# A decode kernel's final store: one transfer of four rows, or two of two rows from two queues

## The chip, the cores and the metric

The kernel runs on one core of a Trainium2 chip. The metric is the device time of one execution in microseconds (us), lower is better; every run quoted as timed was repeated in rounds with the kernel before on the same chip.

Short names used below: PE is TensorE, DVE is VectorE, ACT is ScalarE, POOL is GpSimd, SP is SyncE. "SPq" and "ACTq" are the sequencers of SP and ACT, on which the profile records the issues of DMA transfers. The "record" of an issue is the time that the issuing instruction takes on its sequencer in the profile; a "packet" is one entry of the profile's DMA records (the store of before has four of 512 B); a "count" is one recorded increment of a transfer's semaphore (that store has five).

## The reference, cut to what matters

One decoded token goes through layernorm, and then two branches are added: grouped-query attention over a cache of 65,536 positions, and a small mixer with an MLP. Only the last line, its shape and its size matter here: one row of 1024 bf16 numbers, 2 KB.

```python
x = A_x                                   # (1, 1, 1024)
xn = _layernorm(x, axis=-1)
return x + _A_ref(xn, A_k_cache, A_v_cache, A_wq, A_wo) + _B_ref(xn, B_w1, B_w2, B_w3, B_w4)
```

## The kernel before

Every operation is recorded in a queue for its engine, with the semaphores that it must wait for. `_dma` records a transfer on the queue that issues it; the kernel takes the channel's n-th transfer as done when the channel's semaphore has reached 16 * n. `q_sp.wait` makes SP wait.

```python
def _dma(q, chan, fn, reads=(), writes=(), partial=False):
    _deps(q, reads, writes)               # waits of the issuing queue
    chan.n += 1
    ev = q.dma(fn, chan.sem, 16 * chan.n) # issued by q; "done" is sem >= 16 * n
    _done(ev, reads, writes, partial)
    return ev
```

All final terms are summed in one PSUM tile, `OUT_ps`: the 1024 outputs lie as four rows of 256 in partitions 0, 32, 64 and 96, because the kernel writes each product of one row as four matmuls, each with a `tile_position` of its own.

```python
def out_rows(items, reads, last=False):
    ...
        for jj in range(4):
            ... e.matmul(OUT_ps[32 * jj:32 * jj + 1, 0:256], lhs, rhs[:, 256 * jj:256 * jj + 256],
                         start=False, stop=last, tile_position=(0, 32 * jj), skip_group_check=True)
```

The end of the program waits for the four parts of the weight w4 in turn, adds them, casts the sum to bf16 in `orow`, and stores its four rows with one transfer:

```python
for i in range(len(w4_parts)):
    w4_pe(i)                              # last part: 2 rows of w4, 8 matmuls
_op(q_dve, lambda e: e.tensor_copy(orow[:, :], OUT_ps[:, 0:256]), reads=[b_OUT], writes=[b_orow])
ev_out = _dma(q_sp, chan("out"), lambda e: e.dma_start(
    out=out[0, 0, :].rearrange("(j n) -> j n", j=4), in_=orow[0:97:32, :]), reads=[b_orow])
q_sp.wait(ev_out)
```

ACT issues one transfer in the whole program before the change, the load of x at its start.

## Time and profile before

| | before |
|---|---|
| median of 6 runs | 403.74 us (403.67 to 404.6) |
| span in the profile | 401.93 us |
| HBM read | 169.87 MB at 423 GB/s |
| start of the store's issue to end of span ("the tail") | 2.06 us |

These lines of the page show what bounds the kernel. "DMA" gives the busy share of the DMA engines in 40 equal slices of the span, in tenths.

```profile
span 401.9 us, 5169 instructions
PE 193.7 (48%) x2059; PEld 83.0 (21%) x2059; DVE 227.8 (57%) x400; ACT 48.3 (12%) x127; POOL 61.8 (15%) x90
...
DMA  8999999999999999999999999999999999999994
...
HBM read 169.87 MB, written 0.00 MB: 423 GB/s over the span
```

The DMA engines are busy 90% or more from the second slice to the last but one; no other engine passes 57% of the span. The change touches none of that. What it touches is seen in the chain of waits that ended last (start, length, what):

```profile
374.69 24.24 DMA Kn<-in_B_w_dram
398.93 0.04 issue
398.98 0.42 PE OUT_ps L392 x8
399.39 0.02 issue
399.42 0.42 DVE orow L619
```

and in the timeline of the end (start, length, engine, line, operation):

```profile
399.42 0.42 DVE L619 CAST orow<-OUT_ps 128x256 bf16<-128x256 f32 x1 [13.16 <-PE OUT_ps L392]
399.87 0.65 SPq L620 DMA_DIRECT2D out_dram<-orow  x1
```

The last load lands, eight matmuls and the cast follow, and then there is only the store, over 2 us of it although it moves 2 KB. A table of short windows shows when bytes move in that time; the last two columns are the busy share of the DMA engines and GB/s.

```profile
400.20:401.10 0.90, 0.00 (x0) 0.00 (x0) 0.00 (x0) 0.00 (x0) 0.00 (x0) 1.00 0.00 0
401.10:401.25 0.15, 0.00 (x0) 0.00 (x0) 0.00 (x0) 0.00 (x0) 0.00 (x0) 1.00 0.06 14
401.25:401.50 0.25, 0.00 (x0) 0.00 (x0) 0.00 (x0) 0.00 (x0) 0.00 (x0) 1.00 0.00 0
```

Only the window from 401.10 to 401.25 holds packets. The trace has every packet and every count that arrives at the store's semaphore. Written out from those records, with times from the start of the span:

```
399.870  SP issues the store (record 0.645 us)
400.893  first count: the one that comes ahead of all data
401.120, 401.140, 401.148, 401.180   packets of 512 B, 25 or 26 ns each
401.470, 401.489, 401.498, 401.534   four counts, 0.26 to 0.33 us after the end of the last of these packets
401.551  SP goes on
401.932  end of span, after the closing barrier
```

So 1.25 us pass from the issue to the first packet, 0.09 with packets, 0.33 to the last count, 0.02 to SP and 0.38 in the barrier.

### The profile page before, as it was taken

The page shows a single profiled execution, that of the slowest core. Times are in us where ns is not written, and L with a number is a line of the kernel's source. Part 1 is how long each engine was busy: PE and PEld are TensorE (multiplying, and loading weights), DVE is VectorE, ACT ScalarE, POOL GpSimd, SP SyncE. Part 2 cuts the span into 40 slices and gives each one's busy share as a digit, 9 for nine tenths or more (in the row PEclk, how much of TensorE's full clock was granted, in tenths as well). Part 3 has the DMA queues.
Part 4 walks back from the last instruction along what each step waited for, and adds up shares of the span by engine and source line. Part 5 has one row for each costly group of instructions (what it writes and reads, how often), then busy time and mean ns, then how long its engine had stood idle before and what let it go on. Part 6 is the DMA issues. An engine that isn't in the chain of part 4 may idle for free.

```text
span 401.9 us, 5169 instructions
## 1 busy us (share of the span) xinstructions
PE 193.7 (48%) x2059; PEld 83.0 (21%) x2059; DVE 227.8 (57%) x400; ACT 48.3 (12%) x127; POOL 61.8 (15%) x90
## 2 busy tenths in 40 slices
PE   0361446064525756286640965454443645445645
PEld 0250111021103511062110731121111311111232
DVE  0217666277816588255753388576836775788410
ACT  0000201012101011011110011111201111111200
POOL 5000013011211011110310102111110112112110
PEclk9999999999955565555565556565565855665686
DMA  8999999999999999999999999999999999999994
GB/s 356 427 416 436 444 421 419 450 432 421 444 434 423 432 434 439 416 434 452 423 420 450 426 424 444 432 421 435 430 435 427 445 430 424 424 431 430 436 419 205
DMA packets 7088, 170.20 MB, mean 423 GB/s; under 512 B 916, under 2 KB 920, under 8 KB 1048
## 3 DMA queue, kind: packets, MB, share of 16 engines
q1 hardware_dynamic: 6920, 169.87, 98.4%
q8 instruction: 16, 0.26, 0.2%
q14 instruction: 8, 0.07, 0.0%
q10 hardware_dynamic: 144, 0.00, 0.0%
HBM read 169.87 MB, written 0.00 MB: 423 GB/s over the span
## 4 chain that ended last, share of the span: by engine, by line
DMA 54%; DVE 22%; PE 17%; ACT 3%; issue 2%; SPq 0%; POOL 0%; ACTq 0%
DMA Kn<-in_A_k_cache_dram 43%; DVE X L464 11%; DMA Kn<-in_B_w_dram 6%; DMA Vn<-in_A_wq_dram 5%; PE H_ps L367 4%; DVE pT_f L517 3%; PE S_ps L476 3%; PE OT_ps L524 3%; DVE mrow L483 3%; ACT p_sb L506 3%; PE M_ps L367 2%; PE PT_ps L515 2%; PE M_ps L552 1%; PE OUT_ps L392 1%; DVE Yall L381 1%
## 5 line engine op out<-in xcount | busy, mean ns | idle before, releaser
L464 DVE STREAM_TRANSPOSE X<-Kn 128x1024 f32<-128x1024 f32 x128 | 151.7, 1215 | 64.2 <-DMA Kn<-in_A_k_cache_dram 64.2
L524 PE MATMUL OT_ps<-Vn,pT_f 128*32 128x512 bf16 x512 | 59.9, 620 | 27.2 <-DVE pT_f L517 27.2
L476 PE MATMUL S_ps<-X,Yall 128*32 128x512 bf16 x512 | 57.5, 593 | 17.0 <-DVE X L464 17.0
L489 PE MATMUL MB_ps<-Rm,Lmat 128*128 128x16 bf16 x32 | 6.1, 192 | 87.3 <-DVE Rm L484 87.3
L538 POOL TENSOR_TENSOR O_acc<-O_acc,tmpO 128x513 f32<-128x513 f32 x28 | 32.9, 1174 | 89.0 <-ACT tmpO L532 89.0
L506 ACT ACTIVATE p_sb<-S_ps,brun 128x512 bf16<-128x512 f32 x32 | 22.0, 687 | 172.3 <-DVE brun L504 153.8
L536 POOL TENSOR_SCALAR O_acc<-O_acc,ff 128x513 f32<-128x513 f32 x28 | 19.5, 698 | 149.8 <-ACT ff L511 149.8
L515 PE MATMUL PT_ps<-p_sb,permR 128*128 128x512 bf16 x32 | 18.2, 568 | 39.7 <-ACT p_sb L506 39.7
L483 DVE TENSOR_REDUCE mrow<-S_ps 128x1 f32<-128x512 f32 x32 | 21.6, 674 | 24.2 <-PE S_ps L476 24.2
L532 ACT ACTIVATE tmpO<-OT_ps 128x512 f32<-128x512 f32 x32 | 19.1, 598 | 107.6 <-PE OT_ps L524 107.6
L476 PEld LDWEIGHTS S_ps<-X,Yall 128*32 128x32 bf16 x512 | 16.5, 125 | 54.8 <-DVE X L464 38.6
L517 DVE STREAM_TRANSPOSE pT_f<-PT_ps 128x512 f32<-128x512 f32 x32 | 22.9, 716 | 7.6 <-PE PT_ps L515 7.6
L524 PEld LDWEIGHTS OT_ps<-Vn,pT_f 128*32 128x32 bf16 x512 | 14.5, 127 | 59.2 <-DVE pT_f L517 42.4
L489 PEld LDWEIGHTS MB_ps<-Rm,Lmat 128*128 128x128 bf16 x32 | 3.3, 102 | 111.2 <-DVE Rm L484 111.2
L367 PEld LDWEIGHTS H_ps<-xn_bf,W 128*128 128x128 bf16 x224 | 14.4, 174 | 1.7 <-issue 1.7
L367 PE MATMUL H_ps<-xn_bf,W 128*128 128x1 bf16 x224 | 14.5, 202 | 0.0
L515 PEld LDWEIGHTS PT_ps<-p_sb,permR 128*128 128x128 bf16 x32 | 3.4, 106 | 42.4 <-ACT p_sb L506 42.4
L493 DVE TENSOR_REDUCE Bst<-MB_ps 128x1 f32<-128x16 f32 x32 | 5.6, 174 | 8.3 <-PE MB_ps L489 8.3
L331 PE MATMUL M_ps<-ln_s,ones_f 128*128 128x1 f32 x6 | 1.8, 363 | 17.5 <-DVE ln_s L330 17.5
L534 POOL COPY O_acc<-tmpO 128x513 f32<-128x513 f32 x4 | 2.4, 612 | 47.6 <-ACT tmpO L532 47.6
L392 PE MATMUL OUT_ps<-Kn,gh_bf 128*1 128x256 bf16 x112 | 6.4, 402 | 5.5 <-DMA Kn<-in_B_w_dram 5.5
L619 DVE CAST orow<-OUT_ps 128x256 bf16<-128x256 f32 x1 | 0.4, 425 | 13.2 <-PE OUT_ps L392 13.2
(101 smaller groups left out, 117.3 us busy)
## 6 DMA issues: line engine op xcount, KB each, us to landing
Kn<-in_A_k_cache_dram SPq DMA_DIRECT2D x15, 4096.0 KB, 27.5
Vn<-in_A_v_cache_dram SPq DMA_DIRECT2D x15, 4096.0 KB, 22.2
W<-in_B_w_dram SPq DMA_DIRECT2D x2, 3584.0 KB, 24.9
W<-in_A_wo_dram SPq DMA_DIRECT2D x3, 2048.0 KB, 24.3
Kn<-in_A_wq_dram SPq DMA_DIRECT2D x1, 4096.0 KB, 12.2
Vn<-in_A_wq_dram SPq DMA_DIRECT2D x1, 4096.0 KB, 21.4
W<-in_B_w_dram SPq DMA_DIRECT2D x2, 2048.0 KB, 32.1
Kn<-in_A_k_cache_dram SPq DMA_DIRECT2D x2, 2048.0 KB, 24.9
```

What stands on the lines that cost most here:

```text
L367: fns.append(lambda e, j=j, cx=cx: e.matmul(ps_tile[:, c0 + cx:c0 + cx + 1], lhs_fn(j - j0, cx), rhs_fn(j), start=(j == 0 and cx == 0), st ...
L392: fns.append(lambda e, lhs=lhs, rhs=rhs, jj=jj: e.matmul(OUT_ps[32 * jj:32 * jj + 1, 0:256], lhs, rhs[:, 256 * jj:256 * jj + 256], start=F ...
L464: _op(q_dve, lambda e, ix=ix: e.transpose(out=X32[:, xs, 1024 * ix:1024 * (ix + 1)], in_=Kn32[:, s, 4096 * half + 1024 * ix:4096 * half + ...
L476: fns.append(lambda e, we=we, cm=cm, mv=mv: e.matmul(S_ps[32 * cm:32 * cm + 32, :], Yall[:, h, we, :, :].rearrange("p a g -> p (a g)"), mv ...
L483: _op(q_dve, lambda e: e.reduce_max(mrow[:, m:m + 1], S_ps[:, :], axis=AX.X), reads=[b_S], writes=[b_mrow[m]])
L506: _op(q_act, lambda e: e.activation(p_sb[:, m, :], S_ps[:, :], ACTF.Exp, bias=brun[:, kn:kn + 1], scale=SCALE, accum_out=tmpO[:, m, 512:513]),
L515: _op(q_pe, lambda e: e.matmul(PT_ps[:, :], permR[:, :], p_sb[:, m, :], start=True, stop=True), reads=[b_p[m], b_const], writes=[b_PT])
L517: _op(q_dve, lambda e: e.transpose(out=pT_f[:, :], in_=PT_ps[:, :]), reads=[b_PT], writes=[b_pT])
L524: fns.append(lambda e, q=q, q4=q4: e.matmul(OT_ps[32 * q4:32 * q4 + 32, :], pT_bf[:, q, :, 1], Vn[:, s, 8192 * half + 512 * q:8192 * half ...
L532: _op(q_act, lambda e: e.activation(tmpO[:, m, 0:512], OT_ps[:, :], ACTF.Copy), reads=[b_OT], writes=[b_tmpO[m]], partial=True)
L536: _op(q_pool, lambda e: e.tensor_scalar(out=O_acc[:, :], in0=O_acc[:, :], scalar1=ff[:, m:m + 1], scalar2=0.0, op0=ALU.mult, op1=ALU.add), ...
L538: _op(q_pool, lambda e: e.tensor_tensor(out=O_acc[:, :], in0=O_acc[:, :], in1=tmpO[:, m, :], op=ALU.add), reads=[b_tmpO[m]], writes=[b_Oacc])
```

## The change

The intent is to shorten the store by sharing it between two queues that can issue at the same time (at the start of the trace of before ACT starts an issue at 0.788 us and SP at 0.793): SP stores rows 0 and 1, ACT stores rows 2 and 3. SP waits for both, each on its own semaphore.

```diff
-        ev_out = _dma(q_sp, chan("out"), lambda e: e.dma_start(out=out[0, 0, :].rearrange("(j n) -> j n", j=4), in_=orow[0:97:32, :]), reads=[b_orow])
-        q_sp.wait(ev_out)
+        out_j = out[0, 0, :].rearrange("(j n) -> j n", j=4)
+        for q, j0 in ((q_sp, 0), (q_act, 2)):
+            ev_out = _dma(q, chan("out%d" % j0), lambda e, j0=j0: e.dma_start(out=out_j[j0:j0 + 2, :], in_=orow[32 * j0:32 * j0 + 33:32, :]), reads=[b_orow])
+            q_sp.wait(ev_out)
```

Although the wait stands in the loop, it is SP's alone and comes after SP's own issue, so it does not hold ACT back (in the profile after, ACT's issue starts 4 ns after SP's).

## The prediction

> **What bounds the kernel.** HBM reading: the page shows 169.87 MB read at 423 GB/s over a span of 401.9 us, and the DMA row stands at 9 tenths in all slices but the first and the last; the busiest engine, DVE, has 57%. [...] The chain of waits ends in 24.24 us of the w4 load (landed 398.93), 8 matmuls (0.42), the cast of orow (0.42, ends 399.84), and then only the store. The change touches this store alone, so it can move only the tail of 2.1 us, half a per cent of the time.
>
> **The tail, from the trace's records.** SP issues the store at 399.87 (0.65 us); a first completion count[...] comes at 400.89; four packets of 512 B run from 401.12 to 401.20 (25 ns each); four more counts land at 401.47 to 401.53; SP goes on at 401.55; the closing barrier ends the span at 401.93. Of 1.66 us from issue to last count, 1.25 is issue to first packet, 0.08 moving data, 0.33 completion. Bytes cost nothing here.
>
> **What the change does.** One issue of four rows becomes two of two rows, side by side on SP and ACT. ACT has been idle since its last activation (ended 381.8), so it can issue as soon as orow is cast. [...] Both transfers must be complete, so the tail is the later of two chains with the same fixed 1.6 us.
>
> Gains: if issue time depended on the row count, under 0.1 us; but 128-row loads issue in 0.33 us and this 4-row store took 0.65. Costs: a second wait on SP (estimate 0.03 to 0.06 us, from the 33 ns compare and 17 ns semaphore records); [...] perhaps a hold-up [...] (0 to 0.4). At this trace's start ACT and SP issued at the same instant (0.788 and 0.793) and both took 0.39 us, so I expect little.
>
> Sum: -0.1 to +0.4, centre +0.1 us, all on the critical path; the three runs of before spread 0.9 us.
>
> **Predicted time: 403.9 us, 8 in 10 within 403.2 to 404.8. Faster by over 2%: 0.005; within 2%: 0.985; slower by over 2%: 0.01.**
>
> **What would show it.** Right: two issues within 0.05 us of each other, on SP and ACT, each 0.5 to 0.7 us; cast end to end of span 2.0 to 2.5 us (2.09 now); the w4 load landing within 1 us of 398.9; two late counts for each store. [...] Wrong on fixed cost: a tail under 1.9 us.
>
> **What would make it wrong.** A different pace of the load stream, 99% of the span[...]; an ACT queue slow to start after 400 us of disuse (its x load took 12.4 us to land, but beside the wq loads). Neither should reach 2%, 8 us.

One cost in the forecast's sum is gone, 0.05 us for more packets; the sum, -0.1 to +0.4 us with its centre at +0.1, still includes it. The terms left are the gain (under 0.1 us), the second wait (0.03 to 0.06) and a hold-up (0 to 0.4). The bounds of the gain and of the hold-up were guesses, worked out from no run.

## The result, and the profile after

| | before | after |
|---|---|---|
| median of 6 runs, us | 403.74 | 404.09 (404.02 to 404.29) |
| span in the profile, us | 401.93 | 402.36 |
| tail, us | 2.06 | 2.33 |
| at 2% | | same: ratio 1.0006, 95% interval 0.9994 to 1.0019 |

Here and below the two numbers after a ratio are its 95% interval. Ratios are the mean time of one kernel's fast runs over the mean of the other's fast runs of the same rounds, so not quite the ratio of the two medians.

The direction is seen in the runs: of the six times of before five lie at 403.82 or lower (the sixth is 404.6), and none of the six after lies under 404.02. The page after is the same in all that bounds the kernel:

```profile
span 402.4 us, 5155 instructions
PE 185.8 (46%) x2043; PEld 82.9 (21%) x2059; DVE 227.7 (57%) x400; ACT 48.3 (12%) x127; POOL 61.8 (15%) x90
...
DMA  8999999999999999999999999999999999999994
...
HBM read 169.87 MB, written 0.00 MB: 422 GB/s over the span
```

(That PE counts 16 instructions fewer is taken as a gap in the trace's records: PEld has 2059 in both, and the change touches no matmul.) The chain's end:

```profile
375.52 23.36 DMA Kn<-in_B_w_dram
398.88 0.04 issue
398.93 0.62 PE OUT_ps L392 x8
399.55 0.02 issue
399.58 0.42 DVE orow L619
```

The timeline of the end:

```profile
399.58 0.42 DVE L619 CAST orow<-OUT_ps 128x256 bf16<-128x256 f32 x1 [12.59 <-PE OUT_ps L392]
400.03 0.63 SPq L622 DMA_DIRECT2D out_dram<-orow  x1
400.03 1.34 ACTq L622 DMA_DIRECT2D out_dram<-orow  x1
```

And the short windows:

```profile
400.00:401.20 1.20, 0.00 (x0) 0.00 (x0) 0.00 (x1) 0.00 (x0) 0.00 (x0) 0.50 0.00 0
401.20:401.35 0.15, 0.00 (x0) 0.00 (x0) 0.00 (x0) 0.00 (x0) 0.00 (x0) 0.50 0.03 7
401.35:401.50 0.15, 0.00 (x0) 0.00 (x0) 0.00 (x0) 0.00 (x0) 0.00 (x0) 0.50 0.00 0
401.50:401.60 0.10, 0.00 (x0) 0.00 (x0) 0.00 (x0) 0.00 (x0) 0.00 (x0) 0.50 0.04 10
```

Three things are to be read here.

First, the last load landed as before (its last count came at 398.88 where it had come at 398.93), so the load stream did not change its pace. Second, the eight matmuls took 0.62 us where they took 0.42, and that is 0.2 us of the 0.42 by which the two spans differ. It happens ahead of the change; the experiments return to it. Third, the two issues start together, at 400.028 and 400.032, but the packets come in two clumps with a gap. From the packet and count records of after:

```
400.028  SP issues (record 0.628 us)        400.032  ACT issues (record 1.336 us)
401.219  SP's first count                   401.454  ACT's first count
401.257, 401.277  SP's packets              401.528, 401.544  ACT's packets
401.614, 401.626  SP's counts               401.888, 401.894  ACT's counts
401.911  SP passes the wait for ACT's store
401.967  SP passes the wait for its own
402.356  end of span
```

SP's half has its packet 1.23 us after the issue, as the whole store had before. ACT's half has it 1.50 us after, 0.27 later, and the end waits for it.

Of the four late counts two belong to each store, where the one store of four rows had four (401.470 to 401.534).

### The profile page after: what moved, and what is told of

It reads as the page before. It is cut to its first block, busy times and chain, and to the rows that moved or that the text cites. A ratio compares the mean times of both kernels' runs of the same rounds, so it can differ in the third digit from the quotient of the medians.

```text
span 402.4 us, 5155 instructions
## 1 busy us (share of the span) xinstructions
PE 185.8 (46%) x2043; PEld 82.9 (21%) x2059; DVE 227.7 (57%) x400; ACT 48.3 (12%) x127; POOL 61.8 (15%) x90
## 4 chain that ended last, share of the span: by engine, by line
DMA 54%; DVE 24%; PE 17%; issue 2%; ACT 1%; another core or an unknown queue 1%; SPq 0%; POOL 0%; ACTq 0%
DMA Kn<-in_A_k_cache_dram 43%; DVE X L464 13%; DMA Kn<-in_B_w_dram 6%; DMA Vn<-in_A_wq_dram 5%; PE H_ps L367 4%; PE S_ps L476 3%; DVE pT_f L517 3%; PE OT_ps L524 3%; DVE mrow L483 3%; PE M_ps L367 2%; ACT p_sb L506 1%; PE PT_ps L515 1%; PE M_ps L552 1%; PE OUT_ps L392 1%; DVE Yall L381 1%
## 5 line engine op out<-in xcount | busy, mean ns | idle before, releaser
L515 PE MATMUL PT_ps<-p_sb,permR 128*128 128x512 bf16 x16 | 9.3, 580 | 21.2 <-ACT p_sb L506 21.2
```

Of the source, the lines that this page charges most:

```text
L515: _op(q_pe, lambda e: e.matmul(PT_ps[:, :], permR[:, :], p_sb[:, m, :], start=True, stop=True), reads=[b_p[m], b_const], writes=[b_PT])
```

## The experiments

All times below are from the start of a store's own issue, unless "tail" is named: that is from the first store issue to the end of the span. The theories, guesses for the experiments to tell apart:

- A: of two issues that start together the second is held up by the first, ahead of the DMA engines.
- B: ACT is slow to issue, by itself, with nobody beside it.
- C: a transfer of two rows is slower than one of four.
- D: the two halves wait for each other in the DMA engines.

| run | stores | issue records, us | first packet, us | tail, us | median us, and of before in its rounds |
|---|---|---|---|---|---|
| before | SP 4 rows | 0.645 | 1.250 | 2.06 | 403.74 |
| after | SP 2, ACT 2 | 0.628, 1.336 | 1.229, 1.496 | 2.33 | 404.09, 403.74 |
| ctl_after | the same | 0.632, 1.340 | 1.236, 1.503 | 2.33 | 404.05, 403.78 |
| ctl_before | SP 4 | 0.652 | 1.254 | 2.07 | 403.77, 403.66 |
| act_one4 | ACT 4 | 1.092 | 1.254 | 2.07 | 403.81, 403.78 |
| act_half | ACT 2 (wrong) | 1.079 | 1.238 | 2.00 | 403.70, 403.78 |
| sp_two | SP 2, SP 2 | 0.630, 0.487 | 1.231, 1.132 | 2.63 | 404.27, 403.78 |
| split13 | SP 1, ACT 3 | 0.312, 1.294 | 0.755, 1.458 | 2.30 | 404.03, 403.66 |
| sp_late | ACT 2, SP 2 | 1.080, 0.629 | 1.243, 1.478 | 2.28 | 404.04, 403.66 |
| act_late | SP 2, ACT 2 | 0.629, 1.329 | 1.232, 1.489 | 2.32 | 403.92, 403.66 |
| act_wait | SP 2, ACT 2, 0.63 us later | 0.629, 1.080 | 1.229, 1.239 | 2.69 | 404.41, 403.83 |
| four1 | SP 1 and 1, ACT 1 and 1 | 0.322, 0.249; 0.498, 0.234 | 0.776, 0.725; 0.745, 0.719 | 2.12 | 403.93, 403.83 |
| sp8 | SP, 8 of 2 x 64 columns | 0.623, then 0.47 to 0.49 | 1.224 | 5.70 | 407.47, 403.83 |
| alt8 | SP 4, ACT 4 of the same | 0.632 and 1.340 first | 1.229, 1.495 | 4.73 | 406.36, 403.83 |

The medians are of 6 runs for before and after, of 5 for the others, of 4 for sp8 and alt8; act_half and sp_late were run once, their state is unknown, and their time carries no verdict: of these two only what happens after the store's issue, in one profile each, is used. The profile of each is one execution. The tail repeats well: 2.06 and 2.07 for before; 2.33 and 2.33 for after, and 2.32 for act_late, which turned out to be the same case.

### ctl_after: the change again

Edit: none.

> The changed kernel again, unaltered, to see whether its first profile repeats. Tail = start of the first store issue to end of span: 2.06 us before, 2.35 after. All theories: SP's issue record 0.6 to 0.7 us, ACT's 1.2 to 1.4, ACT's packets 0.2 to 0.35 us after SP's, tail 2.3 to 2.4; time 0.2 to 0.5 us over before. If instead the long ACT record was chance: ACT's record near 0.65 and tail near 2.1.

Records of 0.632 and 1.340 us, ACT's packets 0.271 us after SP's, tail 2.33; 404.05 against 403.78, ratio 1.0009 (0.9996 to 1.0021). The picture repeats. It is no chance of one profile.

### act_one4: the whole store from ACT

```diff
-        for q, j0 in ((q_sp, 0), (q_act, 2)):
-            ...
+        ev_out = _dma(q_act, chan("out"), lambda e: e.dma_start(out=out_j, in_=orow[0:97:32, :]), reads=[b_orow])
+        q_sp.wait(ev_out)
```

> One store of all four rows, issued by ACT alone. Theory A ([...] the second is held up): ACT's issue record falls to 0.6 to 0.7 us, first packet 1.2 to 1.3 us after the issue, tail 2.0 to 2.15, time as before within 0.15. Theory B (ACT is slow to issue by itself, after 400 us without a transfer or always): record 1.2 to 1.4 us, first packet about 1.5 us after the issue, tail 2.3 to 2.4, time 0.2 to 0.4 over before.

Each theory got one half right. The timeline and windows of this kernel:

```profile
400.12 1.09 ACTq L621 DMA_DIRECT2D out_dram<-orow  x1
```

```profile
401.30:401.50 0.20, 0.00 (x0) 0.00 (x0) 0.00 (x0) 0.00 (x0) 0.00 (x0) 0.50 0.04 10
401.55:401.70 0.15, 0.00 (x0) 0.00 (x0) 0.00 (x0) 0.00 (x0) 0.00 (x0) 0.50 0.00 0
```

ACT's record is long even alone, 1.09 us, as B had it. But the first packet comes at 1.254 us, as from SP in ctl_before (1.254), the last count at 1.664 as before, and the tail and the time are those of before (2.07; ratio 1.0002, 0.9989 to 1.0015). So the length of ACT's issue record does not delay the data, and B is no explanation of the change's cost. The reader who takes the 1.34 us bar in the profile after for the cause would be wrong by most of it.

### act_half: ACT's half alone

Rows 0 and 1 are never stored (and the result was wrong).

```diff
-        for q, j0 in ((q_sp, 0), (q_act, 2)):
+        for q, j0 in ((q_act, 2),):
```

> Wrong on purpose: ACT alone stores its two rows, rows 0 and 1 are never stored. Theory A: ACT's record about 0.63 us (as SP's two-row store in the change), first packet at 1.2 to 1.3 us, tail 2.0 to 2.1. Theory B: 1.3 us record, first packet at 1.5. Theory C (a transfer of two rows is itself slower than one of four): first packet or counts later than 1.66 us after the issue although nothing is beside it.

The timeline, and then the short windows:

```profile
399.99 1.08 ACTq L622 DMA_DIRECT2D out_dram<-orow  x1
```

```profile
401.20:401.35 0.15, 0.00 (x0) 0.00 (x0) 0.00 (x0) 0.00 (x0) 0.00 (x0) 0.50 0.03 7
401.45:401.60 0.15, 0.00 (x0) 0.00 (x0) 0.00 (x0) 0.00 (x0) 0.00 (x0) 0.50 0.00 0
```

Record 1.079 us, again long; first packet at 1.238 us; last count at 1.600, tail 2.00. Without company ACT's two rows are 0.06 us quicker to their last count than four rows are (1.600 against 1.664), so C falls. Beside SP's store the same transfer has its first packet at 1.496 and its last count at 1.862: company costs it 0.26 us. This is the cleanest size of the hold-up, since the ACT half is the same in both, though it rests on one profile of act_half.

### sp_two: both halves from SP

```diff
-        for q, j0 in ((q_sp, 0), (q_act, 2)):
+        evs = []
+        for q, j0 in ((q_sp, 0), (q_sp, 2)):
             ev_out = _dma(...)
-            q_sp.wait(ev_out)
+            evs.append(ev_out)
+        for ev_out in evs:
+            q_sp.wait(ev_out)
```

> Two stores of two rows, both issued by SP. Both issues in one queue, so the second starts when the first's record ends, about 0.65 us later, whatever the theory. Theory A: the second's packets come about as late as ACT's did in the change (0.27 us after the first's) or somewhat later, tail 2.3 to 2.7. Theory B: the second pays the full serial issue, packets 0.65 us after the first's, tail 2.7 to 2.9.

The second issue starts 0.677 us after the first, whose record is 0.630, its packets come 0.578 us after the first's, tail 2.63: inside A's range, and close under B's, so this run alone decides nothing between them. It gives the price of splitting on one queue: 404.27 against 403.78, ratio 1.0015 (1.0001 to 1.0028), tail +0.56. Two queues cost half of that, +0.27. The second queue helps against a split; it does not help against not splitting.

### ctl_before: the kernel before, again

Edit: one line that nothing uses (`out_j = ...`); it records no operation.

> The kernel before, unaltered, for a second profile of it. Its first profile had 0.42 us for the last eight matmuls, all five later profiles 0.6; if that belongs to the change, here 0.42 again; if it is the clock granted at that moment, it may be 0.6 here too. Tail (store issue to end of span) 2.0 to 2.1 us, SP's record 0.62 to 0.66, first packet 1.2 to 1.3 after the issue; time within 0.15 of before.

The timeline has 0.60 us for the eight matmuls here, as in after; in before's first profile it has 0.39 (the chains above have 0.62 for after and 0.42 for before). The granted TensorE clock (the column ahead of the DMA share) differs in the same way. The window from 399.00 to 399.60 is shown three times: of before's first profile, of after, and of ctl_before.

```profile
399.00:399.60 0.60, 0.36 (x8) 0.08 (x8) 0.18 (x1) 0.00 (x0) 0.00 (x0) 1.00 0.00 0
```

```profile
399.00:399.60 0.60, 0.52 (x8) 0.03 (x8) 0.02 (x1) 0.00 (x0) 0.00 (x0) 0.50 0.00 0
```

```profile
399.00:399.60 0.60, 0.42 (x8) 0.00 (x0) 0.13 (x1) 0.00 (x0) 0.00 (x0) 0.50 0.00 0
```

With a granted clock of 1.00 the eight matmuls take 0.39 us, with 0.50 they take 0.60, and the unchanged kernel shows both. So the 0.2 us ahead of the cast in the first comparison of the profiles is no part of the change, and the two spans of the result overstate its cost; the tail is the fair measure. Tail 2.07, time 403.77 against 403.66 (ratio 1.0001).

### split13: one row from SP, three from ACT

```diff
-        for q, j0 in ((q_sp, 0), (q_act, 2)):
-            ... out=out_j[j0:j0 + 2, :], in_=orow[32 * j0:32 * j0 + 33:32, :] ...
+        for q, j0, nj in ((q_sp, 0, 1), (q_act, 1, 3)):
+            ... out=out_j[j0:j0 + nj, :], in_=orow[32 * j0:32 * (j0 + nj) - 31:32, :] ...
```

> SP stores row 0 alone, ACT rows 1 to 3. In the change ACT's packets came 1.50 us after its issue, against 1.24 alone. Theory A [...]: all three of ACT's packets come 1.45 to 1.55 after its issue. Theory D (held up in the DMA engines[...]): [...] ACT's three packets are spread over 0.2 us or more instead of 0.05.

The timeline of the two issues, and then the short windows:

```profile
400.04 0.31 SPq L622 DMA_DIRECT2D out_dram<-orow  x1
400.05 1.29 ACTq L622 DMA_DIRECT2D out_dram<-orow  x1
```

```profile
400.75:400.85 0.10, 0.00 (x0) 0.00 (x0) 0.00 (x0) 0.00 (x0) 0.00 (x0) 0.50 0.02 5
401.20:401.45 0.25, 0.00 (x0) 0.00 (x0) 0.00 (x0) 0.00 (x0) 0.00 (x0) 0.50 0.00 0
401.45:401.60 0.15, 0.00 (x0) 0.00 (x0) 0.00 (x0) 0.00 (x0) 0.00 (x0) 0.50 0.04 10
```

SP's packet was there and gone at 400.80, and still ACT's three packets came only at 1.458, 1.464 and 1.483 us after the issue, all together, about 0.2 us later than ACT's four rows alone (1.254). SP's one packet (a packet of 512 B takes 25 or 26 ns in the traces of before and after) cannot have stood in the way of three in the DMA engines 0.7 us after it, and its store was complete, last count and all, at 1.113 us. From 401.20 to 401.45 the DMA share is 0.00, and ACT's packets are spread over 0.025 us, not over 0.2. So D falls: by these records the hold-up lies ahead of the engines.

Not expected by any theory: a store of one row has its packet after 0.755 us instead of 1.23 to 1.25. Bytes are not the reason: the first store of sp8 below has fewer (256 B, in two rows), and its first packet comes after 1.224 us.

### sp_late: who is held up, ACT or the second?

```diff
+        for ev in ((q_pe.sem, q_pe.cnt), *b_orow.w.items(), (q_act.sem, q_act.cnt), (q_pool.sem, q_pool.cnt)):
+            q_sp.wait(ev)                  # (comment of this text) all met by then; they only take SP a little time
         for q, j0 in ((q_sp, 0), (q_act, 2)):
```

> SP gets extra waits, already met, so that it issues about 0.05 to 0.2 us after ACT instead of 4 ns before it. If the one that comes second is held up (A): ACT's packets at 1.2 to 1.3 after ACT's issue, SP's later than 1.3 after its own, or at least behind ACT's. If SP always goes first or ACT is slow beside any other (B'): ACT's packets still at 1.45 or later. Tail 2.2 to 2.45 either way.

The delay came out small, 38 ns, but enough to turn the order round:

```profile
400.03 1.08 ACTq L624 DMA_DIRECT2D out_dram<-orow  x1
400.07 0.63 SPq L624 DMA_DIRECT2D out_dram<-orow  x1
```

Now ACT's packets come at 1.243, as alone, with the record as alone (1.080), and SP's come at 1.478, 0.24 to 0.25 later than in the change, where SP was first. So of two issues 38 ns apart or less it is the second that is held up here, whichever queue it is on; that SP can be the one held up rests on this one profile. One more thing is to be seen: SP's record is 0.629 us although SP is held up, and 0.628 where it is not. The record of an issue need not show a hold-up.

### act_late: a delay that did not delay

```diff
+        _op(q_act, lambda e: e.activation(tmpO[:, 0, 0:512], S_ps[:, :], ACTF.Copy), reads=[b_orow, b_S], writes=[b_tmpO[0]])
         for q, j0 in ((q_sp, 0), (q_act, 2)):
```

> ACT does one activation of 0.6 us between the cast and its issue, so the issues no longer coincide. Theory A: ACT's packets come 1.2 to 1.3 after its own issue, its record is 1.05 to 1.12 us as alone; SP's first count returns from 1.19 to about 1.0 after its issue. Tail 2.0 + about 0.65 delay = 2.6 to 2.8, time 0.5 to 0.8 over before. If ACT is held up merely by SP having issued at all: 1.45 or more, tail 2.9 or more.

The experiment failed. ACT's sequencer issued the store beside the activation, not after it; both start at 400.41:

```profile
400.41 0.60 ACT L621 ACTIVATE tmpO<-S_ps 128x512 f32<-128x512 f32 x1 [17.78 <-DVE orow L619]
400.41 1.33 ACTq L623 DMA_DIRECT2D out_dram<-orow  x1
```

So it is the change once more: packets at 1.232 and 1.489, tail 2.32, and 403.92 against 403.66 (ratio 1.0005, 0.9991 to 1.0019).

### act_wait: the delay mended

```diff
+        q_act.wait(_op(q_act, lambda e: e.activation(tmpO[:, 0, 0:512], S_ps[:, :], ACTF.Copy), reads=[b_orow, b_S], writes=[b_tmpO[0]]))
         for q, j0 in ((q_sp, 0), (q_act, 2)):
```

> The last experiment mended: in act_late ACT's sequencer issued the store beside the activation, not after it, so nothing was delayed. Here ACT's store also waits for that activation's semaphore. ACT then issues 0.6 to 0.75 us after SP. Theory A (the issue that comes second is held up about 0.25 us while the first holds something at its start): ACT's packets 1.2 to 1.3 after its own issue, record 1.05 to 1.12, tail from SP's issue 2.6 to 2.8. If merely having the other store in flight costs 0.26: packets at 1.45 or later, tail 2.9 or more.

The timeline, and then the short windows:

```profile
400.05 0.63 SPq L623 DMA_DIRECT2D out_dram<-orow  x1
400.06 0.60 ACT L621 ACTIVATE tmpO<-S_ps 128x512 f32<-128x512 f32 x1 [17.71 <-DVE orow L619]
400.69 1.08 ACTq L623 DMA_DIRECT2D out_dram<-orow  x1
```

```profile
401.25:401.35 0.10, 0.00 (x0) 0.00 (x0) 0.00 (x0) 0.00 (x0) 0.00 (x0) 0.50 0.04 10
401.35:401.85 0.50, 0.00 (x0) 0.00 (x0) 0.00 (x0) 0.00 (x0) 0.00 (x0) 0.50 0.00 0
401.85:402.00 0.15, 0.00 (x0) 0.00 (x0) 0.00 (x0) 0.00 (x0) 0.00 (x0) 0.50 0.03 7
```

Issued 0.633 us after SP, while SP's store is still in flight (its packets came at 401.28), ACT's store has its first packet 1.239 us after its own issue and a record of 1.080, as if alone. The hold-up is gone. It is therefore not company as such: by then SP's store was in flight, but its issue record had ended, 4 ns before. Where between 0.04 and 0.63 us the hold-up ends, no run of two stores tells (alt8 below has something on it). SP's first count came back as well, to 1.007 us from 1.191. The tail is 2.69 because ACT was made late; the time is 404.41 against 403.83 (ratio 1.0014, 1.0 to 1.0028).

### four1: four single rows, two from each queue

```diff
-        for q, j0 in ((q_sp, 0), (q_act, 2)):
-            ...
+        for j, q in enumerate((q_sp, q_sp, q_act, q_act)):
+            evs.append(_dma(q, chan("out%d" % j), lambda e, j=j: e.dma_start(out=out_j[j:j + 1, :], in_=orow[32 * j:32 * j + 1, :]), reads=[b_orow]))
+        for ev_out in evs:
+            q_sp.wait(ev_out)
```

> Four stores of one row, two from SP and two from ACT. In split13 SP's one-row store had its packet 0.755 us after the issue instead of 1.24. If a single row is always so quick: SP's packets at about 0.75 and 1.1 to 1.2, ACT's first at 0.95 to 1.05 (held up 0.25); ACT's second after its first record, 0.7 to 0.8 us later, at 1.5 to 1.8. Then tail 2.3 to 2.6, no better than before (2.06). If ACT's record too is short for one row (0.35), its second comes at about 1.3 and the tail is 2.0 to 2.15, equal to before.

The timeline (the two issues of each queue are merged in one line):

```profile
400.10 0.61 SPq L623 DMA_DIRECT2D out_dram<-orow  x2
400.11 0.77 ACTq L623 DMA_DIRECT2D out_dram<-orow  x2
```

Single rows are quick from both queues, each packet 0.72 to 0.78 us after its issue. And A's hold-up is not seen: ACT, 4 ns behind SP, has its packet at 0.745 us, before SP's own at 0.776. No run has a single row with nothing beside it, so this is judged against the second row of each queue (0.725 and 0.719). The last count comes 1.643 us after the first issue, 0.02 ahead of the single store (1.664), and SP loses that again with four waits (its last wait passed at 1.738, against 1.681). Tail 2.12, time 403.93 against 403.83, ratio 1.0002 (0.999 to 1.0015): no better than before, and nearer to it than the change is.

So A's hold-up is seen where the second store has two or three rows, and not with two single rows side by side. Why is open.

### sp8 and alt8: eight stores, on one queue or on two

Eight stores of two rows by 64 columns; in sp8 all from SP, in alt8 alternately from SP and ACT. The results are correct.

```diff
-        for q, j0 in ((q_sp, 0), (q_act, 2)):
-            ...
+        for i, q in enumerate((q_sp,) * 8):        # alt8: (q_sp, q_act) * 4
+            j0, c0 = 2 * (i % 2), 64 * (i // 2)
+            evs.append(_dma(q, chan("out%d" % i), lambda e, j0=j0, c0=c0: e.dma_start(out=out_j[j0:j0 + 2, c0:c0 + 64], in_=orow[32 * j0:32 * j0 + 33:32, c0:c0 + 64]), reads=[b_orow]))
+        for ev_out in evs:
+            q_sp.wait(ev_out)
```

> Eight stores of two rows by 64 columns, all from SP. The second store of sp_two came 0.58 us after the first: last packets at 1.24 + 7 x 0.58 = 5.3 us after the first issue, tail about 6.1, time 4 us over before under every theory; the yardstick for alt8.

> The same eight stores, alternately from SP and ACT. Theory A (only about 0.25 us of each issue excludes the other queue): each queue goes at its own pace, ACT's four take 3 x (1.08 to 1.4) + 1.5 = 4.7 to 5.7 us to their last packet, SP's four 3.0 to 3.8: tail 5.5 to 6.5, about that of sp8, because ACT is the slower issuer. If the whole issue excluded the other (0.6 to 1.1 each in turn): last packets after 7 us, tail 8 or more.

sp8: tail 5.70 (expected 6.1), 407.47 against 403.83, ratio 1.0091. After the first two each further issue starts 0.52 us after the one before; the expectation had taken 0.58. alt8: tail 4.73, below both ranges, 406.36 against 403.83, ratio 1.0061. The expectation missed because it gave every store of ACT the long record of 1.08 to 1.34 us, and only the first has it; ACT's next three took 0.50, 0.65 and 0.69. A whole issue in turn (tail 8 or more) is refuted either way.

The packet records of alt8 also show a delay between issues that do not start together: SP's fourth store, issued 0.37 us after ACT's second and 0.16 before ACT's third, has its first packet 1.322 us after its issue, where the fourth of sp8 has it after 1.115. Which of the two neighbours delays it is not shown.

These two show what a second queue does buy: with eight small stores the last issue ends at 3.27 us instead of 4.25, 0.98 earlier, and the tail falls by 0.97, from 5.70 to 4.73. With one store no second issue stands in line.

## Why the prediction was right

The time was forecast at 403.9 with 403.2 to 404.8, within 2%; it came to 404.09. The direction and the place were as forecast. The size, 0.27 us in the tail, lay within the forecast sum (-0.1 to +0.4) but well over its centre of 0.1. The range of the time says little about the mechanism: it was wide enough to hold the kernel before (403.74) as well. Point by point:

- "The change touches this store alone, so it can move only the tail of 2.1 us." Right. The load landed 0.05 us from where it had landed, and the tail moved by 0.27 us. The profile's 0.2 us for slower matmuls lies ahead of it and was shown by ctl_before to be no part of the change; the granted clock differs with it.
- "1.25 is issue to first packet... Bytes cost nothing here." Right for two rows and more: half the bytes had their first packet at 1.23 instead of 1.25 us. It failed for one row (0.755), though not for want of bytes (256 B in two rows: 1.224), which the argument did not need.
- "Gains: if issue time depended on the row count, under 0.1 us." Its size was right: two rows alone are at their last count 0.064 us sooner than four (act_half). The reason given against it, that issue time does not shrink with rows, is wrong for a single row (0.312 against 0.645).
- 0.05 us for more packets. No such cost is seen: two rows from two queues have their packets in two clumps 0.27 us apart, so they never meet. On which engines the packets run is not in the records.
- "a second wait on SP (estimate 0.03 to 0.06 us)". Right: SP passes its two waits 56 ns apart.
- "perhaps a hold-up", 0 to 0.4 us, and "so I expect little." The range held, the expectation in it did not. This is the term that was mis-sized: 0.26 us, nearly the whole cost. The step that failed was reading two issue records of 0.39 us at the start of the trace as a sign of no hold-up. sp_late shows that SP's record stays at 0.629 us while its packets are 0.24 us late. The packets of those two loads, which the prediction did not look at, would not have reassured: in the trace of before SP's first comes 1.04 us after its issue, ACT's 2.91. (ACT's is 2.67 to 2.91 in every profile, also where ACT issues a few ns first, and no run has this load alone: what keeps it is open.)

The sum, from the records: hold-up 0.262, ACT's start behind SP's 0.004, two rows quicker than four -0.064, second wait 0.056; together 0.26 of the 0.27 by which the tail grew. The forecast had a centre of 0.1 with -0.1 to 0.4.

One of its signs for being wrong: an issue of 0.9 us or more, or one store's packets over 0.3 us after the other's. The second did not come up (0.271 us); the first did, ACT's 1.34 us, which also breaks its sign for right, two issues of 0.5 to 0.7 us each. Taken as the size of the hold-up it would have misled: 1.08 us of that is there when ACT is alone and its data is on time. Only the other 0.26 us is the hold-up.

What is shown, for stores of two and three rows: the issue that starts second, 4 to 38 ns after the other, is held up 0.2 to 0.27 us; it is so for ACT in five profiles and for SP in one; it is gone when the issues are 0.63 us apart; and it is not in the DMA engines (split13). What holds the second issue up is not shown, nor why two single rows (four1) do not hold each other up.

Also open is why ACT's first store has so long a record. Alone, ACT's store of two or four rows takes 1.08 to 1.09 us to issue with no delay of its packets, and its later ones (alt8, two rows of 64 columns) 0.50 to 0.69; whether the 400 us without a transfer or being the first is what counts is not shown. From the end of the issue record to the first packet it was 0.60 to 0.61 us for SP's undisturbed first stores of two and four rows, and 0.16 us for ACT's (act_one4, act_half).

## What to carry to other kernels

The small store at the end of this program takes 1.66 us from issue to last count, of which 0.09 us has packets; half of it alone takes 1.60 (act_half). Two stores of two rows side by side cost that 1.60 us, plus a wait (0.056 us) and a hold-up (0.26): where bytes are not the cost, as here, look for no gain from splitting; none of the forms tried here had any. A second queue paid when eight issues stood in line on one sequencer (a tail of 4.73 us against 5.70), not when there was one. To judge a transfer, look at its packets and its completion counts; the bar of its issue can be long without delaying anything (ACT's 1.09 us in act_one4), and can hide a delay (SP's 0.63 us in sp_late).
